# A new order table for a fused gated-linear-attention and gated-MLP kernel

## The chip, the cores and the metric

The kernel runs on one core of a Trainium2 chip. A core has five engines with an instruction queue each: TensorE (PE; the profile shows its weight loads apart, as PEld), VectorE (DVE), ScalarE (ACT), GpSimd (POOL) and SyncE (SP), which here issues the transfers. The metric is the device time of one execution in microseconds (us), as the median of several runs. Beside it one execution was profiled; its time from the first to the last instruction is the span.

## What is computed

The first half is a linear recurrence over 768 steps, for 4 batches and 8 heads of width 48:

```python
for t in range(S):
    state = alpha[:, :, t, :, None] * state + np.einsum('bhd,bhe->bhde', k[:, :, t], v[:, :, t])
    y[:, :, t] = np.einsum('bhd,bhde->bhe', q[:, :, t], state)
```

Its result, with the heads side by side as x (4 x 768 x 384), goes through a gated MLP with a product over the sequence:

```python
h = np.maximum(x @ w_in, 0.0)
u, v = (h[..., :d_ff // 2].copy(), h[..., d_ff // 2:].copy())
v_n = (v - mu) / np.sqrt(var + 1e-06)
v_s = np.einsum('ts,bsd->btd', w_spatial, v_n) + b_spatial[None, :, None]
out = (u * v_s) @ w_out
```

mu and var are taken over the 512 columns of v. All inputs and the output are 32-bit floats; the kernel multiplies in bf16.

## The kernel before

**The recurrence** is done in chunks of 128 steps, 24 of them (6 for each batch), all heads together. For a chunk the kernel takes the logarithm of alpha (ACT, `ln`), sums it up along the steps with a product by a triangle of ones (PE, `cum`, line 618), and forms both exponentials on ACT (`einv`, `eexp`). k is multiplied by one (`kt`, line 642, on POOL or DVE), q by the other (`qt`, line 652, on DVE). PE transposes both (`trk`, line 671), ACT or DVE copies them out of PSUM (`ev`), PE multiplies q and k to scores (`sc`, line 706), DVE masks these (`m`, line 717), and PE multiplies them by v and adds the state's part (`y`, line 734 and 728). The state goes on from chunk to chunk through DVE and POOL (`z`, `S`, `sb`). The first eight chunks are done as four pairs of chunks with functions of their own (`pair`): there the steps are called `lnp`, `cump` (line 406), `totp` (line 423), `einvp`, `eexpp`, `ktp` (442), `qtp` (449), `tr` (470), `updq` (505), `sc` (535), `m` (546), `ya` (562), and a transfer brings 384 KB in place of 192.

**The MLP** takes over when a chunk is through. Its rows are copied (`xs`), transposed (`xt`), copied out (`xe`). Then PE computes `v` (x by one half of w_in, 512 columns), and for each half batch of 384 rows `u` (the other half, transposed), all of them in line 780. DVE or ACT takes v's statistics (`bn`, `rs`) and normalises it (`vn`, line 877 on DVE, 886 on POOL). PE multiplies by w_spatial (`s`, two parts of three products), DVE adds the bias (line 928, tile vsb), POOL or DVE multiplies by u (`g`, line 941, tile gT), PE multiplies by w_out (`o`), ACT or DVE copies the result (line 148 or 150) and SP stores it (line 999). The very last product of the table's numbering comes in two half-width pieces (`oh`, line 963), one of which ACT stores (line 972). For the last `s` of all, line 921 multiplies by u straight from PSUM.

**What sets the order.** No engine decides at run time. The functions only collect operations: each has a key, the engines that can do it, what it needs, and a function that emits it. Then `replay` walks through the string PLAN (line 57): one word for each of 1160 operations, with the letter of the engine that does it (P, D, A, G for POOL, S for a transfer's issue, Q for the transfer itself) and its number. Each engine gets its instructions in the order of the words and works through them strictly in that order; semaphores make it wait where data or a buffer are not there. So the table decides two things: which of its possible engines does an operation, and what stands behind what in each engine's queue. A planner outside the kernel wrote it.

Numbers behind a P word's colons are columns of filler: products of a constant tile (`junk`, line 138) that go out ahead of that operation into the bank that it will use, and whose results are never read.

```python
for word in plan.split():
    number, *junk = word[1:].split(":")
    op, eng = ops[int(number)], LETTERS[word[0]]
    fill.extend(int(x) for x in junk)
    op.emit(eng)
```

The weights come by six transfers of 768 KB (w_in in two halves, w_spatial in three parts, w_out) through two raw buffers, and are cast in pieces to bf16 (line 150 on DVE and POOL, 148 on ACT): a raw buffer's next transfer waits for these casts. Loads of q, k, v and alpha go through three buffers each, in SP's order.

Of the kernel before, what the change touches and what calls it, by code (L numbers as in the profile page):

```python
# [54 lines left out]
LETTERS = {"P": "PE", "D": "DVE", "A": "ACT", "G": "POOL", "S": "SP", "Q": "DMA"}  # L55

PLAN = """
S110 Q111 D0 D17 D5 G47 Q48 D3 D6 D1 S49 Q50 D11 D2 D15 S53 Q54 D13 D12 G14 D4 A118 S51 Q52 G16 A57 S55 Q56 P119:192:64:128:192:320:192:192:64 G9 P58 S114 Q115 G8 A59 P68:64 A60 D61 S112 Q113 A69 P129:256 D62 A120 P70 G72 A71 S180 Q181 A130 P66:384 D73 A121 P64:64 D63 P131 A80 A74 S116 Q117 D123 A132 P79:64 A65 D134 A67 P127 S182 Q183 P75 A141 D81 D122 P138:128 G82 P77 A139 P265 D78 A76 S184 Q185 G18 A266 D84 P125:128 A128 P87 A126 P90 D88 A188 P148 G133 D92 S19 Q20 P199:64:128 A124 D89 P189 G135 A200 G85 D91 S186 Q187 P136:256 G83 P201 D149 P140 A202 G203 D150 A211 S325 Q326 A190 P93 A137 D142 P97 A191 G192 D204 A94 P206:64:128 D193 P208 A98 G143 P95 A209 P195 S24 Q25 P99 G144 A96 D145 D100 P197:64 D196 G22 P151 A198 P267 A207 D153 G21 A23 P215 D152 P218 G86 A268 S327 Q328 P104 D217 G146 P154 A105 D219 G147 S329 Q330 P155 A194 P101 D216 G205 A156 D7 P159 D220 G10 A102 P210 D160 A333 P221 S29 Q30 D212 P157 D103 P161 S331 Q332 G213 P222 A158 P344 A223 G214 P163 D162 A345 D106 G28 P224 P226 A164 P346 D225 G27 P334 A347 D227 P174 G26 A107 D165 P228 A356 P230 A175 G109 S33 Q34 D229 A335 S386 Q387 P166 D176 A336 G348 P245 D349 A177 P233 D338 G337 A246 P170 A231 D167 P243 G31 A171 D232 P353 A32 P340 G178 P351 D234 P239 A354 S37 Q38 A244 P342 D235 P172 A240 S388 Q389 G350 A341 P168 G339 D173 A352 A343 G179 A236 P247:64 S390 Q391 P250 A169 D248 P366 D108 A251 P241 A252 D367 S392 Q393 G35 A249 P355 A242 D368 G238 A394 P253 P363 D254 A255 P395 D357 P273 D237 A397 G358 A396 D365 P281 A36 D360 P282 S432 Q433 D364 A40 P274 D283 S41 Q42 G398 P277 A399 D275 P278 S428 Q429 D400 G39 P256 P262 D279 P402 A258 G359 A264 P269 D276 A403 A404 P270 G284 A257 A263 S430 Q431 A401 P259 P409 D261 P369 D260 G361 D271 P373 P293 A374 D411 P285 S499 Q500 D280 P294 D370 P375 P405 S465 Q466 G45 D410 P297 G272 P298 D406 S467 Q468 A436 P286 A376 G407 D299 P371 G362 P437 D295 A372 P380 A438 D43 D287 A439 A441 P412 G440 S434 Q435 P289 A381 D442 P290 A413 G300 S471 Q472 P444 P414 S469 Q470 P377 G296 A473 D416 D415 D445 A446 P426 A507 D291 G46 S501 Q502 P420 A378 D382 G408 P451 S503 Q504 A443 G44 P474 D421 P508 A427 P447 D379 A476 P417 S596 Q597 A509 G480 A475 D452 P309 A478 G477 S505 Q506 A418 D453 P301 A511 D479 P424 S598 Q599 G510 A310 D448 P454 A302 S600 Q601 A425 P422 D512 G288 A383 D455 P481 A423 P514 G449 D482 P456 A483 P305 D457 G292 A515 D419 A516 P484 A458 S602 Q603 A306 P488 D485 P517 A604 D490 P459 G486 S667 Q668 A513 D519 G450 P605 A460 P313 S669 Q670 D489 G487 A606 P317 D518 A607 A609 G608 S630 Q631 A314 P491 D461 P520 A492 S709 Q710 G611 P321 D610 A521 G384 D318 P493 S632 Q633 P612 A495 D494 P522 A462 P615 D613 P496 D523 A614 D524 G464 A675 D322 P532 A497 P525 S634 Q635 D533 A498 D385 P619 A526 D616 S713 Q714 P534 D463 A527 P536 D621 S671 Q672 A638 P538 D528 A717 P548 D620 A529 S711 Q712 P676 A535 P718 D531 P639 A677 D530 S673 Q674 P544 A719 D537 G679 P622 A720 A640 P549 D539 S636 Q637 A641 A678 A722 P545 G642 D550 A680 P564 D723 S715 Q716 A643 P565 G617 A623 D681 P552 S751 Q752 D546 G721 P553 D644 S781 Q782 G618 D566 P624 P683 A625 P646 D684 G551 P556 A645 D648 S747 Q748 P557 A626 D554 A647 G547 A685 P649 S749 Q750 A682 D558 P653 P690 D650 P725 D655 S785 Q786 P540 G651 A726 A727 D691 P560 G652 A789 P561 D654 G555 A724 P541 D692 P686 S783 Q784 G567 P568 D687 D542 P693 S753 Q754 A755 G559 P656 D562 A694 P569 A657 S877 Q878 G688 P756 D570 P695 G543 P658 A757 P732 D696 S883 Q884 D697 A758 P790 A760 D734 P627 G689 A659 A660 A791 D761 S787 Q788 P580 A793 D733 G792 A628 P728 S881 Q882 P661 D729 D730 G759 P735 D794 A662 P572 D581 A736 G731 D663 A885 P796 P737 S879 Q880 P763 G571 A739 P698 A738 D797 A764 D573 A765 S915 Q916 P701 G563 D798 P740 D629 S911 Q912 A702 G762 A699 P770 G892 P799 A664 D772 S990 Q991 P766 G795 A741 P584 D771 G665 S917 Q918 P886 A585 D801 P576 A887 S913 Q914 D767 P588 A888 A890 D800 G889 A742 P705 D577 A589 G768 P773 D891 P896 G769 D706 A774 P707 S590 Q591 A919 D666 P775 S948 Q949 P893 A776 D777 P802 A708 D894 S1027 Q1028 P592 A895 D897 A700 G926 P703 S950 Q951 D593 A803 P900 A998 D743 P804 P778 A805 D902 A806 S992 Q993 A744 P807 D901 A779 G746 S952 Q953 P817 A704 D780 A956 P815 S994 Q995 G898 A808 P999 D745 G899 P957 A816 D809 P819 A959 A958 S1029 Q1030 P821 A818 D960 P825 A1001 A810 S954 Q955 P813 A1000 D812 A961 P920 D811 S1065 Q1066 P829 A1003 D962 A922 P830 A921 D1004 S1061 Q1062 A820 P826 G923 D831 A814 P822 A1035 D827 S996 Q997 P903 G832 A924 D823 P930 P833 A904 D931 A963 G828 P834 D925 D932 P905 P927 S1031 Q1032 G1002 A906 P964 D835 A928 P967 A966 P849 D965 S1033 Q1034 A929 D907 P850 D836 S1063 Q1064 D968 P1006 D824 P971 G969 A1007 P934 D851 A1069 P908 G970 A1008 D972 P1036 A909 P853 D1005 D973 A1037 P841 A1038 A854 D935 G1039 P1009 A1040 P842 S855 Q856 D936 S594 Q595 P837 G933 D1041 S311 Q312 P937 D1010 S1067 Q1068 P838 D843 A938 G1042 P1070 D839 P1043 A1071 P1013 D1045 P939 A1073 P845 G1072 D1014 A940 A1044 P846 D1074 G1011 P974 D1015 P861 G844 A975 D847 A941 P1076 A862 D910 P976 G848 P1046 A1077 P1016 A977 A978 D1078 P942 A1017 G1075 D1047 G1012 P1018 P1050 D1019 A1020 P1079 A943 D1051 G840 P986 D1080 P857 D1048 P1021 D1081 G1049 P979 D1052 A1022 G852 P1082 A987 D858 P1053 D944 S859 Q860 P988 A1054 S307 Q308 P865 A1083 D980 S574 Q575 A945 S863 Q864 P1084 D1023 P1055 P984 A1085 G946 S586 Q587 A989 P982 S303 Q304 A1057 D1056 A866 D1086 D981 S315 Q316 P869 S582 Q583 P1087 A1024 A983 P1095 D1025 A1088 D947 P1058 D1026 A985 D1089 P1093 A1059 P1097 A1096 D870 P1101 A1094 D1060 S871 Q872 A1098 P1109 S319 Q320 P1105 A1090 S867 Q868 P873 D1091 D1092 P1121 P1106 P1102 D1107 P1122 D1103 P1113 D1108 P1114 D1123 P1117 D1115 G1124 P1110 D1104 P1099 G1116 P1118 D1111 A1100 P1125 A874 D1119 G1112 P1126 S875 Q876 P1129 S323 Q324 D1127 G1120 S578 Q579 P1130 P1132 D1131 G1128 P1140 A1133 P1152 S1134 Q1135 D1141 P1144 A1153 S1142 Q1143 P1136 A1145 S1154 Q1155 P1148 S1146 Q1147 D1137 P1156 S1138 Q1139 A1149 A1157 S1150 Q1151 A1158 Q1159
"""


# [1065 lines left out]
```

## Time and profile before

| what | value |
|---|---|
| median of 3 runs | 139.31 us (139.02 to 139.58) |
| span of the profiled execution | 137.4 us |
| PE busy | 132.7 us, 97% of the span |
| DVE busy | 116.1 us, 84% |
| ACT busy | 101.3 us, 74% |
| POOL busy | 92.9 us, 68% |
| filler on PE (line 138) | 11.4 us busy in 44 records |
| transfers | 28.64 MB, 208 GB/s on average |
| mean granted clock of PE | 0.995 |

How to read what the prediction quotes. A row of a group has the line, engine and operation, what it writes and reads with its shape and count, then busy us and mean ns of one; behind a second bar stands the engine's idle time ahead of these instructions and what ended it. A row of the timeline has the start and the length in us, then the same names; x3 at its end are three instructions merged. Products on PE overlap, so the time of one record is longer than the pace at which they follow one another. A row of the chain of waits has the start, the length and the work that held the end of the program at that time.

### The profile page before, as it was taken

What the parts mean: (1) busy time and instruction counts of PE and PEld (TensorE: products, weight loads), DVE (VectorE), ACT (ScalarE), POOL (GpSimd) and SP (SyncE); (2) the same over time, 40 slices, a digit from 0 to 9 for tenths busy, and PEclk for the clock granted to TensorE, in tenths of its full rate; (3) what the DMA queues carried; (4) which work ended last, traced back from release to release, by engine and by line L of the source; (5) the groups of instructions that cost most, each with busy time, mean ns of one, the idle gap of its engine ahead of it and who ended that gap; (6) DMA issues with size and microseconds to landing.
All of it is one profiled execution on the core that took longest, in us unless ns stands there. A gap on an engine that the chain in (4) does not pass through costs nothing.

```text
span 137.4 us, 5023 instructions
## 1 busy us (share of the span) xinstructions
PE 132.7 (97%) x1943; PEld 88.4 (64%) x1943; DVE 116.1 (84%) x278; ACT 101.3 (74%) x286; POOL 92.9 (68%) x165
## 2 busy tenths in 40 slices
PE   6999999999999999999999999999999999999990
PEld 6768885757667655775667665656666666555660
DVE  7157989998998979998899999989999989878640
ACT  3488687999874799989974887999966757760241
POOL 4734998899894898793399999825666785202910
PEclk9999999999999999999999999999999999999998
DMA  3999999998979899899998989999994602940355
GB/s 95 319 322 328 275 343 328 331 293 243 319 120 314 160 193 203 166 208 193 207 210 160 212 168 199 196 200 212 193 183 114 169 10 108 350 171 6 130 188 197
DMA packets 89000, 28.64 MB, mean 208 GB/s; under 512 B 83728, under 2 KB 87440, under 8 KB 88976
## 3 DMA queue, kind: packets, MB, share of 16 engines
q1 hardware_dynamic: 88800, 28.22, 83.8%
q8 instruction: 15, 0.25, 0.7%
q10 hardware_dynamic: 144, 0.10, 0.2%
q14 instruction: 9, 0.07, 0.1%
q0 software_dynamic: 32, 0.00, 0.0%
HBM read 23.60 MB, written 4.72 MB: 206 GB/s over the span
## 4 chain that ended last, share of the span: by engine, by line
PE 95%; ACT 1%; issue 1%; DVE 0%; ACTq 0%
PE bank L780 58%; PE bank L138 7%; PE bank L671 3%; PE bank L706 3%; PE bank L470 3%; PE bank L734 2%; PE bank L618 2%; PE bank L692 2%; PE bank L535 2%; PE bank L728 2%; PE bank L406 2%; PE bank L343 2%; PE bank L505 2%; PE bank L562 1%; PE bank L320 1%; PE bank L792 1%
## 5 line engine op out<-in xcount | busy, mean ns | idle before, releaser
L780 PE MATMUL bank<-w_spT,vn 128*128 128x384 bf16 x192 | 35.1, 326 | 0.0
L941 POOL TENSOR_TENSOR gT<-vsb,uT 128x384 bf16<-128x384 f32 x25 | 22.8, 928 | 9.2 <-DVE vsb L928 8.6
L780 PEld LDWEIGHTS <-vn 128*128 128x128 bf16 x192 | 17.5, 97 | 10.5
L717 DVE TENSOR_TENSOR ptm<-bank,mask 128x512 bf16<-128x512 f32 x32 | 20.6, 681 | 0.1
L642 POOL TENSOR_TENSOR kt<-kc,binv 128x384 bf16<-128x384 f32 x15 | 13.9, 932 | 9.6 <-ACT binv L630 5.4
L780 PE MATMUL bank<-xT,w_in 128*128 128x384 bf16 x96 | 19.4, 326 | 0.0
L780 PE MATMUL bank<-w_in,xT 128*128 128x512 bf16 x72 | 19.2, 379 | 0.0
L928 DVE TENSOR_TENSOR vsb<-bank,bsp_bc 128x384 f32<-128x384 f32 x31 | 16.6, 552 | 2.0 <-PE bank L780 1.6
L780 PE MATMUL bank<-w_out_sb,gT 128*128 128x384 bf16 (+1 forms) x100 | 18.2, 319 | 0.0
L158 ACT ACTIVATE uT<-bank 128x384 bf16<-128x384 f32 x25 | 11.9, 495 | 5.5 <-PE bank L780 5.5
L150 POOL CAST sbd<-state 64x192 bf16<-64x192 f32 x40 | 13.7, 344 | 2.6 <-DVE state L290 0.5
L845 DVE BATCH_NORM_STATS2 stats<-v_sb 128x6 f32<-128x512 bf16 x20 | 13.7, 686 | 0.2
L148 ACT COPY kqT<-bank 128x256 f32<-128x256 f32 x35 | 11.8, 387 | 2.6 <-PE bank L671 1.7
L158 ACT ACTIVATE v_sb<-bank 128x512 bf16<-128x512 f32 x18 | 10.8, 598 | 3.1 <-PE bank L780 2.6
L290 POOL TENSOR_TENSOR state<-state,bc 128x192 f32<-128x192 f32 x17 | 9.5, 559 | 4.9 <-DVE state L283 2.6
L780 PEld LDWEIGHTS <-w_in 128*128 128x128 bf16 x96 | 8.7, 97 | 6.1
L138 PE MATMUL bank<-junk 128*128 128x64 f32 (+5 forms) x44 | 11.4, 389 | 1.1 <-DVE junk L1012 1.1
L780 PEld LDWEIGHTS <-gT 128*128 128x128 bf16 x100 | 8.9, 97 | 5.4 <-POOL gT L941 0.4
L148 ACT CAST x_sb<-bank 128x384 bf16<-128x384 f32 x20 | 9.4, 490 | 3.3 <-PE bank L734 2.3
L546 DVE TENSOR_TENSOR ptm<-bank,mask 128x512 bf16<-128x512 f32 x16 | 10.0, 682 | 0.5 <-PE bank L535 0.5
L612 ACT ACTIVATE la<-ac 128x384 bf16<-128x384 f32 x16 | 8.4, 533 | 2.5 <-DMA ac<-in_alpha_dram 2.5
L138 PEld LDWEIGHTS bank<-junk 128*128 128x128 f32 x44 | 8.8, 242 | 2.0 <-DVE junk L1012 1.1
(133 smaller groups left out, 290.7 us busy)
## 6 DMA issues: line engine op xcount, KB each, us to landing
ac<-in_alpha_dram SPq DMA_DIRECT2D x16, 192.0 KB, 4.6
kc<-in_k_dram SPq DMA_DIRECT2D x16, 192.0 KB, 4.0
qc<-in_q_dram SPq DMA_DIRECT2D x16, 192.0 KB, 3.9
vc<-in_v_dram SPq DMA_DIRECT2D x16, 192.0 KB, 3.9
raw_w<-in_moe_w_spatial_dram SPq DMA_DIRECT2D x3, 768.0 KB, 4.7
out_dram<-raw_w SPq DMA_DIRECT2D x11, 192.0 KB, 2.0
out_dram<-o_sb SPq DMA_DIRECT2D x9, 192.0 KB, 1.9
ac<-in_alpha_dram SPq DMA_DIRECT2D x4, 384.0 KB, 4.6
```

Source lines behind the costliest of these rows:

```text
L138: nc.tensor.matmul(out=flat[:, 0:cols].rearrange("p (a b) -> p a b", a=4), lhsT=junk, rhs=junk[:, None, 0:n].to_broadcast([128, 4, n]), st ...
L148: nc.scalar.copy(out=out, in_=in_)
L150: ENG[eng].tensor_copy(out=out, in_=in_)
L158: nc.scalar.activation(out=out, in_=in_, func=AF.Relu)
L290: ENG[eng].tensor_tensor(out=st["state"], in0=st["state"], in1=st["bc"][:, :, None].to_broadcast([128, HP, D]), op=ALU.mult)
L546: nc.vector.tensor_tensor(out=st[f"ptm{par}"][:, s], in0=st[f"pt{s}{par}"], in1=mask2[:, par], op=ALU.mult)
L642: ENG[eng].tensor_mul(out=k_blocks(kt3)[:, :, :, 0:D], in0=quad(st["kc"]), in1=st["binv"])
L717: nc.vector.tensor_tensor(out=st["ptm"][:, s], in0=st[f"pt{s}"], in1=mask4, op=ALU.mult)
L780: return lambda ps: nc.tensor.matmul(out=out(ps), lhsT=lhsT(), rhs=rhs(), start=start, stop=stop)
L845: nc.vector.bn_stats(out=stats, in_=d["v_sb"][:, tt, :])
L928: nc.vector.tensor_tensor(out=hold["vs"], in0=ps[:, 0:TH], in1=bsp_bc[:, th, :], op=ALU.add)
L941: ENG[eng].tensor_tensor(out=bt[b]["gT"][:, dsl, cols], in0=hold["vs"], in1=bt[b]["uT"][:, dsl, cols], op=ALU.mult)
```

## The change

PLAN is replaced by another table over the same 1160 operations. Nothing else in the program is different. The new table was planned with the rule that DVE and POOL exclude each other while they multiply two SBUF tensors, and with filler in most of PE's early gaps. The diff is one line of words removed and one added; their beginnings:

```diff
-S110 Q111 D0 D17 D5 G47 Q48 D3 D6 D1 S49 Q50 D11 D2 D15 S53 Q54 D13 D12 G14 D4 A118 S51 Q52 G16 A57 S55 Q56 P119:192:64:128:192:320:192:192:64 G9 P58 S114 Q115 G8 A59 P68:64
...
+D0 G47 D1 D13 G14 D4 D15 D7 S49 Q50 A57 P58:512:512:48 S110 Q111 A118 D17 G18 D3 G16 S51 Q52 A59 S53 Q54 S112 Q113 P68 A69 S114 Q115 S55 Q56
...
```

Of the words, 114 name another engine than before (33 go from DVE to ACT, 33 from ACT to DVE, 20 from POOL to DVE, 17 from DVE to POOL, 6 from ACT to POOL, 5 from POOL to ACT); the others only stand elsewhere. On DVE the evacuations of u go from 7 to 12, those of o from 10 to 7, and the vn from 15 to 12; POOL's vn go from 9 to 12. Filler goes from 22 products of 3200 columns (1344 of them in one block at the start) to 7 of 1936 (1072 at the start, then 112, 240, 448 and 64 ahead of single operations).

PE's queue at the start of the program, before. Here junk is the filler, la the logarithm of alpha of a pair of chunks (108 the second pair, 107 the first), le_pair and lt_pair the triangles:

```order
L138 MATMUL bank_85<-junk 128x192
L138 MATMUL bank_85<-junk 128x64
L138 MATMUL bank_85<-junk 128x128
L138 MATMUL bank_85<-junk 128x192
L138 MATMUL bank_85<-junk 128x320
L138 MATMUL bank_85<-junk 128x192 x2
L138 MATMUL bank_85<-junk 128x64
L406 LDWEIGHTS le_pair
L406 MATMUL bank_85<-la_108,le_pair 128x384
```

and now:

```order
L138 MATMUL bank_85<-junk 128x512 x2
L138 MATMUL bank_85<-junk 128x48
L406 LDWEIGHTS le_pair
L406 MATMUL bank_85<-la_107,le_pair 128x384
L406 LDWEIGHTS lt_pair
L406 MATMUL bank_85<-la_107,lt_pair 128x384
```

The filler block is shorter by 272 columns, and the first cumulative sum behind it is that of the first pair, where it was that of the second.

DVE's queue where w_in arrives, before. ptm is a masked score, kqT a copy of transposed q or k, xT one of the MLP's input, state the recurrence's state:

```order
L285 TENSOR_TENSOR state<-bank_85,state 128x192
L150 COPY xT<-bank_87 128x384
L150 COPY kqT<-bank_90 128x512
L546 TENSOR_TENSOR ptm<-bank_85,mask_118 128x512
L546 TENSOR_TENSOR ptm<-bank_92,mask_118 128x512
L546 TENSOR_TENSOR ptm<-bank_88,mask_118 128x512
L546 TENSOR_TENSOR ptm<-bank_89,mask_118 128x512
L546 TENSOR_TENSOR ptm<-bank_87,mask_118 128x512
L200 MEMSET ones_col 128x1
L546 TENSOR_TENSOR ptm<-bank_90,mask_118 128x512
```

and now:

```order
L285 TENSOR_TENSOR state<-bank_87,state 128x192
L150 CAST w_in_103<-raw_w 128x512
L546 TENSOR_TENSOR ptm<-bank_91,mask_118 128x512
L150 COPY kqT<-bank_90 128x512
L546 TENSOR_TENSOR ptm<-bank_92,mask_118 128x512
L546 TENSOR_TENSOR ptm<-bank_89,mask_118 128x512
L546 TENSOR_TENSOR ptm<-bank_91,mask_118 128x512
L150 CAST x_sb<-bank_92 128x384
L546 TENSOR_TENSOR ptm<-bank_88,mask_118 128x512
L285 TENSOR_TENSOR state<-bank_86,state 128x192
L546 TENSOR_TENSOR ptm<-bank_90,mask_118 128x512
```

DVE now casts one third of w_in's first half, which POOL or ACT did, and six masks stand behind that cast, with a copy, a cast and a state update among them.

DVE's queue at the end of the program, before. vsb is the spatial product with its bias, gT its product with u, raw_w and o_sb are output tiles:

```order
L928 TENSOR_TENSOR vsb_122<-bank_88,bsp_bc 128x384
L928 TENSOR_TENSOR vsb_123<-bank_85,bsp_bc 128x384
L928 TENSOR_TENSOR vsb_124<-bank_87,bsp_bc 128x384
L921 TENSOR_TENSOR gT<-bank_88,uT 128x384
L150 COPY raw_w<-bank_90 128x384
L150 COPY o_sb<-bank_85 128x384
```

and now:

```order
L928 TENSOR_TENSOR vsb_122<-bank_92,bsp_bc 128x384
L928 TENSOR_TENSOR vsb_123<-bank_86,bsp_bc 128x384
L941 TENSOR_TENSOR gT<-vsb_122,uT 128x384
L928 TENSOR_TENSOR vsb_124<-bank_88,bsp_bc 128x384
L921 TENSOR_TENSOR gT<-bank_87,uT 128x384
L941 TENSOR_TENSOR gT<-vsb_124,uT 128x384
L150 COPY raw_w<-bank_85 128x384
```

Two of the last products with u, which POOL did, are DVE's now, one of them behind the direct product. On PE the two half-width output pieces come third and fourth of the last seven output products, where they came third and last, and a whole tile is last.

2 lines of the change are left out of this document (1 added, 1 removed).

## The prediction

> **What bounds the kernel now.** I read the page first, then the busy time by stretches, then the chain of waits in order of time, and last the timelines of the start, of the arrival of w_in and of the end.
>
> ```profile
> span 137.4 us, 5023 instructions
> PE 132.7 (97%) x1943; PEld 88.4 (64%) x1943; DVE 116.1 (84%) x278; ACT 101.3 (74%) x286; POOL 92.9 (68%) x165
> PE 95%; ACT 1%; issue 1%; DVE 0%; ACTq 0%
> ```
>
> TensorE (PE) is busy for 97% of the span and holds 95% of the chain that ended last; no other engine holds more than a hundredth of it. The busy time by stretches (from and to in us, the length, then each engine's busy us and its instructions):
>
> ```profile
> 0.00:6.20 6.20, 5.15 (x17) 4.72 (x18) 3.23 (x20) 2.80 (x3) 3.50 (x14) 1.00 0.73 194
> 6.20:32.00 25.80, 25.43 (x478) 18.86 (x476) 21.61 (x49) 21.73 (x57) 20.46 (x40) 1.00 1.10 322
> 32.00:116.00 84.00, 84.00 (x1332) 54.07 (x1330) 78.59 (x183) 68.27 (x204) 63.20 (x106) 1.00 0.87 181
> 80.00:104.00 24.00, 24.00 (x358) 15.00 (x356) 22.83 (x55) 21.36 (x66) 16.21 (x28) 1.00 0.96 191
> 116.00:137.40 21.40, 18.14 (x124) 10.72 (x121) 12.69 (x29) 8.54 (x25) 5.76 (x7) 0.97 0.50 182
> ```
>
> From 32 to 116 us PE has no idle time: 84.00 us busy out of 84.00. Another order can win nothing there except stalls hidden inside busy records. What is left to win lies ahead of 32 us and behind 116 us. The chain says what PE did there (the first row is the share of each line, the others start, length and work):
>
> ```profile
> by line: PE bank L780 58.1%; PE bank L138 6.6%; PE bank L671 3.2%; PE bank L706 3.1%; PE bank L470 2.7%; PE bank L734 2.3%; PE bank L618 2.2%; PE bank L692 2.2%; PE bank L535 2.0%; PE bank L728 1.8%; PE bank L406 1.6%; PE bank L343 1.6%; PE
> 1.05 5.17 PE bank L138 x16
> 6.22 0.84 PE bank L406 x4
> 20.64 0.76 PE bank L535 x32
> 21.40 0.75 PE bank L780 x3
> 116.64 17.18 PE bank L780 x105
> ```
>
> L138 is the filler. It holds 6.6% of 137.4, 9.07 us: one block of 5.17 us until 6.22, and 3.9 us in small pieces behind that. The first attention product (cumulative sums, L406) starts at 6.22 and the first product with w_in (L780) at 21.40. The last stretch of products runs from 116.64 for 17.18 us, to 133.8. So the profiled time is 6.2 us of start, 3.9 of filler, 0.4 of idle (25.80 less 25.43), 123.3 of products, and 3.6 of end.
>
> **What the change leaves.** In the order PE's list differs by its fillers alone: 3821 rows before, 3806 now, and every other form stands there as often as it did. Fillers go from 22 instructions of 3200 columns to 7 of 1936. Since the 123.3 us of products stay, the sum is made of four terms: the start, the time around w_in's arrival, the middle and the end.
>
> **Start.** Two forms of filler (busy us, then the mean ns of a record), SP's first transfers and ACT's first logarithms:
>
> ```profile
> L138 PE MATMUL bank<-junk 128*128 128x320 f32 x2 | 1.3, 741 | 0.0
> L138 PE MATMUL bank<-junk 128*128 128x384 f32 x2 | 0.9, 528 | 0.0
> 0.74 1.04 SPq L386 DMA_DIRECT2D ac<-in_alpha_dram  x2
> 4.25 0.84 ACT L397 ACTIVATE la<-ac 128x768 bf16<-128x768 f32 x1 [2.23 <-DMA ac<-in_alpha_dram]
> 5.53 0.84 ACT L397 ACTIVATE la<-ac 128x768 bf16<-128x768 f32 x1 [0.44 <-DMA ac<-in_alpha_dram]
> ```
>
> Before, 1344 columns of filler take 5.17 us, 3.85 ns each; the new block has 1072, so 4.1 us, and ends near 5.2. Two alpha transfers are first on SP in both tables, so the first logarithm again ends at 4.25 + 0.84 = 5.09, and the first cumulative sum starts near 5.2 where it was 6.22. This lead of 1.0 us is worth 0.0 by itself, for what comes behind it hangs on transfers.
>
> **The arrival of w_in.** SP's list has the same eleven 384 KB transfers ahead of the first w_in, in another order (kc ahead of qc, vc of pair 0 behind kc and qc of pair 1). So w_in lands when it did:
>
> ```profile
> 20.06 1.17 POOL L150 CAST w_in<-raw_w 128x512 bf16<-128x512 f32 x2
> 20.43 3.69 DVE L546 TENSOR_TENSOR ptm<-bank,mask 128x512 bf16<-128x512 f32 x6
> 20.60 0.64 ACT L148 CAST w_in<-raw_w 128x512 bf16<-128x512 f32 x1
> 21.33 0.82 PE L780 MATMUL bank<-w_in,xT 128*128 128x512 bf16 x3
> ```
>
> Before, POOL casts two thirds one after the other (to 21.23) and ACT the last (to 21.24); the product follows at 21.33. Now POOL, ACT and DVE cast one third each. If they start between 19.7 (an estimate: 0.4 before POOL's start) and 20.06, the product follows at 20.4 to 20.8, a lead of 0.5 to 0.95 us; I take 0.75. Against it stands what PE has not done by then: two score products of pair 2 (L535 x32, 0.76 us) lay ahead of the first w_in product and now lie behind it. 0.75 - 0.76 is 0.0: at the same time as much work is left.
>
> From there PE hardly idled before, so it can only lose. DVE casts w_in ahead of six masks. They took 3.69 us from 20.43; now they start near 20.9 with a copy, a cast and a state update between, and the last ends near 25.0 in place of 24.1. PE has two w_in products (0.75 each) and two cumulative sums (0.84) ahead of the product that reads that mask: 2.3 us of cover for 0.9. POOL casts w_in ahead of the state casts (sbd) for which pair 1's second products wait. For such waits I take +0.15, with -0.4 (the best lead kept, the 0.4 of idle gone, less some wait) and +0.9 (DVE's delay bare) as ends.
>
> **The middle.** The exclusion concerns products of two SBUF tensors. These are the rows of gT on both engines (min, median and max ns), and two evacuations that move:
>
> ```profile
> L941 POOL TENSOR_TENSOR gT<-vsb,uT x25: 910/916/1231, 40.3 to 130.2; 128x384 bf16<-128x384 f32 x25
> L941 DVE TENSOR_TENSOR gT<-vsb,uT x6: 544/550/1175, 40.5 to 126.7; 128x384 bf16<-128x384 f32 x6
> L160 DVE TENSOR_SCALAR uT<-bank 128x384 bf16<-128x384 f32 x7 | 3.7, 545 | 0.4 <-PE bank L780 0.4
> L877 DVE TENSOR_SCALAR vn<-v_sb,mvs,rstd 128x512 bf16<-128x512 bf16 x15 | 5.9, 421 | 1.8 <-ACT rstd L870 1.8
> ```
>
> The medians lie at the minima: few of these were stretched, and PE idled for none. So the new rule buys 0 on the path. The order gives DVE twelve evacuations of uT for seven (5 x 0.545 = +2.7 us) and three vn fewer (-1.3). Between 80 and 104 us DVE is busy for 22.83 of 24, so little of this finds room there. I take +0.1; the ends are -0.4 (as much hidden stall gone as the idle seen ahead of 32 us, an estimate) and +1.4 (all of DVE's surplus on the path).
>
> **The end.** DVE's and ACT's last work, and the stores' time to landing:
>
> ```profile
> 127.68 1.03 DVE L928 TENSOR_TENSOR vsb<-bank,bsp_bc 128x384 f32<-128x384 f32 x2
> 130.34 0.56 DVE L921 TENSOR_TENSOR gT<-bank,uT 128x384 bf16<-128x384 f32 x1 [0.58 <-PE bank L780]
> 133.85 0.70 ACT L148 COPY raw_w<-bank 128x384 f32<-128x384 f32 x2 [0.82 <-PE bank L780]
> 134.58 0.38 ACTq L972 DMA_DIRECT2D out_dram<-raw_w  x1
> out_dram<-o_sb SPq DMA_DIRECT2D x9, 192.0 KB, 1.9
> out_dram<-raw_w ACTq DMA_DIRECT2D x1, 96.0 KB, 1.9
> ```
>
> A whole output tile is last now, where half a one was: one copy of about half a us and a store of 1.9 replace two copies in 0.70 and a store of 1.9: +0.05. The half tiles are earlier, and they need all four blocks of gT, of which DVE writes one last, behind the direct product (L921, then L941). Behind PE's last spatial product that is about 0.1 to release, 0.47 (the pace of 1.03 for two), 0.55, and 0.1 again: 1.2 us. PE covers it with two whole output tiles, 8 x 0.164 = 1.3 us (17.18 for 105). It just fits, and one more delay breaks it. In all I take +0.15, with 0 and +0.6 (a gT of 1175 in place of 550).
>
> By the Trainium skill (SBUF — State Buffer, "SBUF: two separate sides") a VectorE operation with two SBUF inputs and a GpSimd operation that reads SBUF exclude each other for a whole instruction; the trace agrees where 1175 stands beside 544. By that rule DVE's earlier gT would wait here for one of POOL's, and the end would be some +0.45, for 140.0 in all.
>
> **Sum.** 0.0 + 0.15 + 0.1 + 0.15 = +0.4 us. The profiled span of 137.4 becomes 137.8; the median of the runs is 139.31, so 1.9 us lie around the span, and the forecast is 139.7 us. About 0.5%, 0.7 us, is what a measurement of this kernel can tell from no change: the forecast is one that it can't.
>
> **Rivals.** *The filler was real time (faster).* The small pieces shrink from 1856 columns to 864, 2.1 us less at the old 3.9 for 1856. If the scores that were put off fit into that time, the lead at w_in's product is 0.95 and nothing new waits, the time is 139.3 - 1.0 = 138.3. For it: those pieces lay in the chain. Against it: work was put off, and the transfers come no earlier. 0.20.
>
> *PE stays slow for longer (slower).* 320 columns of filler in the first block take 741 ns, 384 columns later 528: PE ran slowly at first. The new block is 1.1 us shorter, and behind it PE waits for logarithms and exponentials with little filler. If the slow pace lasts until pair 1's sums are through and some us on, two pairs' cumulative sums (0.84 each two) cost 1.7 more and the small products with them about 0.9, an estimate. Of these 2.6 us the 2.1 of filler saved hide most; 0.5 stay, so 140.2. It decides where rows behind 6.5 us still show the slow pace. 0.12.
>
> By the Trainium skill (TensorE: Matmul & The Clock Gate, "What's actually happening") about 3.4 us of sustained work open the clock, counted in a window that runs free. By that rule a block of 4.1 us may miss a whole window; no run shown here has one so short.
>
> *VectorE becomes the wait (slower).* If the surplus of 1.4 us falls into the stretch from 80 to 104, masks come late, products wait, and the chain grows by as much: 140.7. For it: 1.17 us of room there. Against it: the order spreads these evacuations. It decides where DVE's work in that stretch passes 24 us. 0.18.
>
> **Numbers.** The forecast has 0.50: 0.46 of it within 0.7 us of 139.3, 0.02 on either side. Faster: 0.20 + 0.02 = 0.22. Slower: 0.18, 0.10 of the slow start, and 0.02: 0.30. Same: 0.48, the other 0.02 of the slow start in it. The range is 138.4 (some of the first rival left out) to 140.9 (just above the last).
>
> **What would show it.** Right: w_in's first product near 20.6 with 32 score products behind it, PE without idle from 32 to 116, PE's end within 0.5 us of where it was. Wrong: idle on PE behind 32 us, the slow pace behind 6.5, w_in cast well before 19.7, or dense products unbroken from much before 28 us.

## The result and the profile after

The new table is a little slower: 140.23 us (median of 20 runs) beside 139.22 (20 runs). The medians are 1.0 us apart; the ratio, 1.0059 with a 95% interval of 1.0035 to 1.0083, puts the loss at 0.8 us. Executions more than 1.5% above the fastest of the same kernel are left out of the ratios, here and below. From here on *before* and *after* are the two tables.

The page of after: span and instructions, the engines' busy time, and the shares of the chain that ended last.

```profile
span 138.4 us, 4947 instructions
PE 130.3 (94%) x1901; PEld 82.9 (60%) x1913; DVE 118.3 (86%) x281; ACT 101.4 (73%) x285; POOL 94.3 (68%) x166
PE 73%; DVE 9%; SPq 8%; DMA 4%; ACT 2%; issue 2%; POOL 1%; POOLq 0%; DVEq 0%; ACTq 0%
```

The span is 1.0 longer. PE held 95% of the chain of before; now it holds 73%, and DVE 9%, which had less than 1%. The stretches of after:

```profile
6.20:32.00 25.80, 23.44 (x449) 15.71 (x450) 22.88 (x51) 22.04 (x61) 17.73 (x35) 1.00 1.12 331
32.00:116.00 84.00, 82.75 (x1309) 53.63 (x1316) 79.85 (x184) 67.75 (x198) 64.79 (x108) 1.00 0.92 203
80.00:104.00 24.00, 23.73 (x352) 15.05 (x353) 22.59 (x54) 20.60 (x62) 17.68 (x31) 1.00 0.99 210
```

PE now idles for 1.25 us between 32 and 116, where it had none. Part of that is no idle: 12 of the 72 products of L780 with 512 columns have no record in this trace. So the loss is read off another way: when the same product ends in both traces, set against the products that PE has done by then, counted at the paces at which they follow each other in both.

| mark | before | after | lost up to here |
|---|---|---|---|
| first cumulative sum of chunk 8 ends | 36.83 | 37.86, with 0.94 us more products done | 0.09 |
| attention of chunk 23 ends | 114.85 | 117.02, with 1.32 more | 0.85 |
| last product of the program ends | 134.14 | 135.01 | 0.87 |
| span | 137.4 | 138.4 | 0.95 |

The product of the first mark, in the timeline of before and then of after (start and length in us):

```profile
36.50 0.34 PE L618 MATMUL bank<-la,ut_ones 128*128 128x384 bf16 x1
```

```profile
37.53 0.33 PE L618 MATMUL bank<-la,ut_ones 128*128 128x384 bf16 x1
```

Up to 37 us nothing much was lost, then 0.76 until 117, and behind that 0.10. Where w_in arrives, after does what was forecast. The three casts and the first product with w_in, in the timeline of after:

```profile
19.45 0.62 ACT L148 CAST w_in<-raw_w 128x512 bf16<-128x512 f32 x1
19.45 0.43 DVE L150 CAST w_in<-raw_w 128x512 bf16<-128x512 f32 x1 [0.24 <-DMA raw_w<-in_moe_w_in_dram]
19.48 0.86 POOL L150 CAST w_in<-raw_w 128x512 bf16<-128x512 f32 x1
20.40 0.81 PE L780 MATMUL bank<-w_in,xT 128*128 128x512 bf16 x3
```

Behind 38 us the chain shows where the end was set. Its pieces in after from 73 to 79 us (start, length, work):

```profile
73.19 0.56 DVE vsb L928
...
74.00 2.16 DVE ptm L717 x4
...
76.32 0.54 DVE vsb L928
76.86 0.26 DVE state L285
77.12 0.47 DVE vsb L928
77.59 0.60 DVE gT L941
78.19 0.48 DVE vsb L928
```

For nearly all of 5.5 us the end hung on DVE's queue. By the ends of consecutive products PE waited here for 0.13 (at 73.5), 0.11 (74.1) and 0.19 us (79.1), and elsewhere for 0.14 (41.9) and 0.18 (111.1); ahead of 38 us it waited 0.41 at the transposes of w_spatial (L792, 35.8), without which after would have stood 0.32 better than before there. Before had four waits over 0.04 us behind 38, 0.29 in all.

All of these waits of after, but for the one at 111.1, end when an operation of DVE does. At 111.1 PE waits for POOL: the transposes of kt start 0.06 us behind the end of POOL's second kt (110.89), here and in the traces of x9, x13 and x14 below. In the timeline of after:

```profile
108.99 1.90 POOL L642 TENSOR_TENSOR kt<-kc,binv 128x384 bf16<-128x384 f32 x2
...
110.95 0.29 PE L671 MATMUL bank<-ident,kt 64*128 64x64 bf16 x8
```

What stands ahead of two of these waits, in the timeline of after: DVE and POOL at the same time.

```profile
33.37 1.24 DVE L150 CAST vbp<-vc 128x384 bf16<-128x384 f32 x2
33.39 1.00 POOL L150 CAST w_row<-raw_w 128x768 bf16<-128x768 f32 x1
34.86 0.87 DVE L150 COPY w_spT<-bank 128x384 bf16<-128x384 bf16 x3
35.78 0.35 PE L792 MATMUL bank<-ident,w_row 64*128 64x64 bf16 x12 [0.27 <-DVE w_spT L150]
...
71.94 2.10 POOL L941 TENSOR_TENSOR gT<-vsb,uT 128x384 bf16<-128x384 f32 x2 [0.35 <-DVE vsb L928]
72.11 1.16 DVE L642 TENSOR_TENSOR kt<-kc,binv 128x384 bf16<-128x384 f32 x1
```

The same operations by minimum, median and maximum (ns), in after:

```profile
L941 POOL TENSOR_TENSOR gT<-vsb,uT x24: 907/916/1260, 39.7 to 129.8; 128x384 bf16<-128x384 f32 x24
L642 POOL TENSOR_TENSOR kt<-kc,binv x14: 912/916/1225, 38.6 to 109.9; 128x384 bf16<-128x384 f32 x14
L941 DVE TENSOR_TENSOR gT<-vsb,uT x7: 541/548/799, 45.2 to 131.6; 128x384 bf16<-128x384 f32 x7
L642 DVE TENSOR_TENSOR kt<-kc,binv x2: 548/854/1159, 53.8 to 72.1; 128x384 bf16<-128x384 f32 x2
L290 DVE TENSOR_TENSOR state<-state,bc x2: 734/742/750, 18.0 to 109.4; 128x192 f32<-128x192 f32 x2
L150 DVE CAST vbp<-vc x2: 348/662/977, 33.4 to 33.6; 128x384 bf16<-128x384 f32 x2
```

Two of these rows in before:

```profile
L290 DVE TENSOR_TENSOR state<-state,bc x3: 348/408/605, 80.3 to 113.0; 128x192 f32<-128x192 f32 x3
L150 POOL CAST vbp<-vc x4: 506/509/512, 15.1 to 33.4; 128x384 bf16<-128x384 f32 x4
```

One kt takes 1159 in place of 548, one cast 977 in place of 348, the state updates 742 where before had one at 348. So the exclusion that the table was planned with did not keep the two engines apart on the chip. Before had collisions as well (gT of 1175 in place of 544, at 40.5 us), but PE shows no wait behind those.

### The profile page after: what moved, and what is told of

Same layout as the page of the kernel before. It is cut to its first block, busy times and chain, and to the rows that moved or that the text cites. A ratio compares the mean times of both kernels' runs of the same rounds, so it can differ in the third digit from the quotient of the medians.

```text
span 138.4 us, 4947 instructions
## 1 busy us (share of the span) xinstructions
PE 130.3 (94%) x1901; PEld 82.9 (60%) x1913; DVE 118.3 (86%) x281; ACT 101.4 (73%) x285; POOL 94.3 (68%) x166
## 4 chain that ended last, share of the span: by engine, by line
PE 73%; DVE 9%; SPq 8%; DMA 4%; ACT 2%; issue 2%; POOL 1%; POOLq 0%; DVEq 0%; ACTq 0%
PE bank L780 51%; SPq L386 8%; DMA kc<-in_k_dram 4%; PE bank L706 3%; PE bank L671 3%; PE bank L734 2%; PE bank L692 2%; PE bank L618 2%; PE bank L728 2%; DVE ptm L717 2%; PE bank L343 1%; DVE vsb L928 1%; DVE stats L845 1%; PE bank L562 1%; DVE vbp L150 1%
## 5 line engine op out<-in xcount | busy, mean ns | idle before, releaser
L780 PE MATMUL bank<-w_spT,vn 128*128 128x384 bf16 x192 | 35.1, 326 | 0.1
L780 PEld LDWEIGHTS <-vn 128*128 128x128 bf16 x192 | 17.4, 97 | 10.6
L717 DVE TENSOR_TENSOR ptm<-bank,mask 128x512 bf16<-128x512 f32 x32 | 20.4, 679 | 0.0
L780 PE MATMUL bank<-xT,w_in 128*128 128x384 bf16 x96 | 18.8, 326 | 0.0
L780 PE MATMUL bank<-w_out_sb,gT 128*128 128x384 bf16 (+1 forms) x100 | 18.4, 319 | 0.0
L780 PE MATMUL bank<-w_in,xT 128*128 128x512 bf16 x60 | 16.9, 379 | 1.1 <-issue 0.2
L158 ACT ACTIVATE v_sb<-bank 128x512 bf16<-128x512 f32 x20 | 11.7, 593 | 2.5 <-PE bank L780 2.5
L780 PEld LDWEIGHTS <-w_in 128*128 128x128 bf16 x96 | 8.8, 97 | 6.2 <-DVE xT L150 0.2
L780 PEld LDWEIGHTS <-gT 128*128 128x128 bf16 x100 | 8.7, 97 | 4.8 <-DVE gT L941 0.2
L148 ACT CAST x_sb<-bank 128x384 bf16<-128x384 f32 x18 | 8.5, 482 | 3.3 <-PE bank L734 2.3
L158 ACT ACTIVATE uT<-bank 128x384 bf16<-128x384 f32 x20 | 9.5, 493 | 1.5 <-PE bank L780 1.5
L886 POOL TENSOR_SCALAR vn<-v_sb,rstd,nb 128x512 bf16<-128x512 bf16 x12 | 9.3, 772 | 1.2
L780 PEld LDWEIGHTS <-xT 128*128 128x128 bf16 x72 | 6.1, 98 | 5.7 <-ACT xT L148 0.4
L148 ACT COPY o_sb<-bank 128x384 f32<-128x384 f32 x7 | 3.3, 478 | 7.9 <-PE bank L780 7.9
```

The lines of the kernel that those rows point to most:

```text
L148: nc.scalar.copy(out=out, in_=in_)
L158: nc.scalar.activation(out=out, in_=in_, func=AF.Relu)
L717: nc.vector.tensor_tensor(out=st["ptm"][:, s], in0=st[f"pt{s}"], in1=mask4, op=ALU.mult)
L780: return lambda ps: nc.tensor.matmul(out=out(ps), lhsT=lhsT(), rhs=rhs(), start=start, stop=stop)
```

## Experiments

Three theories. *Collisions*: DVE is late where its SBUF operations overlap POOL's and are stretched, and PE waits for it. *Load*: DVE has too much to do since the evacuations of uT moved there. *Order*: PE's own sequence is worse, whatever DVE does. Later two questions on the start joined: what the filler does (cover, real time, or the clock), and whether the start's lead is worth anything. Each kernel was timed beside runs of before on the same chip (medians 139.17 to 139.51). "Clock" is the number of executions with a mean granted clock under 0.99.

| kernel | median us | ratio to before (95%) | PE's last product ends | clock |
|---|---|---|---|---|
| after | 140.23 | 1.0059 (1.0035 to 1.0083) | 135.01 | 5 of 20 |
| x1, vbp on POOL | 140.34 | 1.0040 (1.0018 to 1.0062) | 134.28 | 2 of 12 |
| x2, gT late | 140.94 | 1.0114 (1.0090 to 1.0139) | 135.67 | 0 of 5 |
| x3, both | 140.53 | 1.0077 (1.0050 to 1.0105) | 134.82 | 4 of 11 |
| x6, uT on ACT | 140.54 | 1.0094 (1.0069 to 1.0120) | 135.32 | 0 of 6 |
| x9, vbp on POOL, kt earlier | 139.36 | 1.0014 (0.9986 to 1.0042) | 134.17 | 2 of 12 |
| x10, x9 with the old filler | 141.88 | 1.0190 (1.0154 to 1.0225) | 136.90 | 0 of 6 |
| x4, before with the new filler | 141.06 | 1.0101 (1.0069 to 1.0134) | 137.26 | 3 of 11 |
| x5, after with the old filler | 142.69 | 1.0227 (1.0195 to 1.0259) | 137.51 | 0 of 6 |
| x11, after, old first block | 140.07 | 1.0055 (1.0031 to 1.0079) | 134.81 | 1 of 11 |
| x12, before, new first block | 139.79 | 1.0022 (0.9991 to 1.0052) | 133.93 | 0 of 12 |
| x13, x9 with two edits more | 139.45 | 1.0008 (0.9984 to 1.0033) | 134.88 | 0 of 12 |
| x14, after with two fillers more | 140.04 | 1.0050 (1.0022 to 1.0078) | 134.77 | 0 of 12 |

(One execution of x3, at 702 us, is no time of this program and is left out of its ratio.) Before has 1 of 89.

### x1: the vbp casts back on POOL

```diff
-P250 D350 P247 D339 A36
+P250 G350 P247 G339 A36
```

> The kernel after, with pair 3's two casts vbp on GpSimd again (one letter each). In the trace of after they lie on VectorE from 33.37 for 1.24 us, one of them 0.98 us long where the fastest of its form takes 0.35, while GpSimd casts w_row from 33.39; TensorE then waits 0.41 us at the w_spT transposes (L792) near 35.8. Collision theory (TensorE lost its 0.8 us in waits for VectorE where VectorE's SBUF operations are stretched beside GpSimd's): that wait falls below 0.15, TensorE's last product ends 0.2 to 0.4 earlier than 135.0, the time is 139.8 to 140.0 beside 140.2. Load theory (VectorE has too much work, 118.3 us busy): VectorE is relieved of 1.2 us and the same is gained. Order theory (TensorE's products stand in a worse order, whatever VectorE does): the wait stays, 140.2.

The timeline of x1 at the same place:

```profile
32.85 0.82 POOL L150 CAST w_row<-raw_w 128x768 bf16<-128x768 f32 x1
33.62 1.02 POOL L150 CAST vbp<-vc 128x384 bf16<-128x384 f32 x2
35.01 0.52 PE L792 MATMUL bank<-ident,w_row 64*128 64x64 bf16 x24
```

The 24 transposes that after did in two halves, with the wait between them, are one record again: the 0.41 is gone, and so is the 0.14 at 41.9. PE's last product ends 0.73 earlier, of which 0.15 was there ahead of this place already. The waits from 73 us on stayed as they were. The median did not fall with the profiled execution, which was the fastest of the twelve; over all executions the ratio is 0.2% lower, inside the interval. Both theories expected this gain, so x1 alone does not choose between them.

Five traces with vbp still on DVE gave a scale for the collision without being made for it, since POOL's cast started at slightly different times in each:

| trace | stretched vbp cast, ns | it ends behind POOL's cast by, us | end to end over the wait in L792, ns |
|---|---|---|---|
| after | 977 | 0.21 | 459 |
| x6 | 922 | 0.21 | none here; 0.22 us of wait ahead of the first of these transposes |
| x2 | 859 | 0.21 | 344 |
| x11 | 794 | 0.21 | 275 |
| x14 | 489 | 0.21 | none |

DVE's cast does not run slower, it waits: whenever POOL's cast ended, it was through 0.21 later. In after, x2 and x11, with the same operations of DVE ahead, PE's wait follows the cast: 118 ns less of cast is 115 less of wait, 65 less is 69 less, and at 489 (x14) there is none. In after POOL's own cast took 1005 ns, in the other four 822 to 827, so the collision can hold both sides. By the Trainium skill (SBUF — State Buffer, "SBUF: two separate sides") the port pair that DVE and POOL share is an exclusive lock for a whole instruction, and a DVE operation contends for it with two SBUF inputs or in a 2-port performance mode; that the cast is held until POOL's is through agrees. A cast has one input, so by that rule it would be in such a mode, which no trace here shows.

### x2 and x3: POOL's two gT behind the state update

```diff
-D566 G567 A626 ... P649 G547 P690 ... D650 A726 D691 D692 P560 S323 Q324 G651 D654 D655 G652
+D566 A626 ... P649 P690 ... D650 A726 D691 D692 P560 S323 Q324 G651 D654 D655 G652 G567 G547
```

> The kernel after, with two gT products of GpSimd (batch 1) put behind its next state update and casts, so that they no longer run beside VectorE's kt of chunk 15 (72.11, 1.16 us where the other kt takes 0.55). No engine changes, VectorE's list is the same word for word. Collision theory: kt takes 0.55 to 0.6, TensorE's waits at 73.5, 74.1 and 79.1 (0.13, 0.11, 0.19) go, its last product ends 0.2 to 0.4 earlier, the time is 139.8 to 140.0. Load theory: VectorE's work is the same and nothing is gained, 140.2. Order theory: 140.2.

The timeline of x2, with the kt and what followed it:

```profile
71.86 0.55 DVE L642 TENSOR_TENSOR kt<-kc,binv 128x384 bf16<-128x384 f32 x1
...
76.60 0.56 DVE L928 TENSOR_TENSOR vsb<-bank,bsp_bc 128x384 f32<-128x384 f32 x1 [0.88 <-POOL gT L941]
...
79.01 0.81 PE L780 MATMUL bank<-w_in,xT 128*128 128x512 bf16 x2 [0.53 <-DVE vsb L928]
```

The collision was gone (0.55), PE had no wait at 73.5 and 74.1, and behind them it stood 0.24 better against after than ahead of 73. Then the edit's own price came: a late gT keeps the vsb that it reads, DVE waited 0.88 for that buffer with everything behind it in its queue, and PE waited 0.38 and 0.59, and 0.40 once more at 116. The first half of the expectation came true, the sum did not; as a fix the edit is worthless. But DVE's list is the same word for word, so the 0.24 is the collision's alone. The same two edits together:

> The kernel after with both edits, the vbp casts on GpSimd and the two gT products behind the state update. Collision theory: 0.5 to 0.7 us of the 0.8 come back, 139.5 to 139.7, TensorE's last product near 134.4. Load theory: the vbp part alone, 139.9. Order theory: 140.2.

x3 shows the sum of both: no wait at L792, none at 73.5, and x2's new ones near 79.

### x6: the uT evacuations back on ACT

```diff
-D242 ... D427 ... D535 ... D818 ... D814 ... D987 ... D1094 ... D1096
+A242 ... A427 ... A535 ... A818 ... A814 ... A987 ... A1094 ... A1096
```

> The kernel after with the eight evacuations of uT that went from ScalarE to VectorE back on ScalarE; the three that went the other way stay on ScalarE too, so VectorE has four. VectorE is relieved of 8 x 0.53 = 4.2 us, ScalarE has 8 x 0.43 = 3.4 more. Load theory: the lost 0.8 comes back, 139.4 to 139.6. Collision theory: the collisions at 33.4, 72.1 and 109.4 are not touched; -0.2 to +0.3, 140.0 to 140.5. Order theory: 140.2.

DVE was relieved (114.9 us busy in place of 118.3) and the kernel is not faster: 1.0094. The waits at 73.5, 74.1, 79.1 and 111 stood as in after. At L792, where DVE had one evacuation less ahead of the stretched cast (922 ns), the wait was 0.22 in place of 0.41: there the stretch and the added evacuation made the wait together. That is nearly all that the relief gained. ACT, with more to do, became late in its turn, and from 95 us on x6 is behind after. The timeline of x6:

```profile
95.34 0.32 PE L618 MATMUL bank<-la,ut_ones 128*128 128x384 bf16 x1 [0.32 <-ACT la L612]
```

So the load theory falls as an account of the 0.8 us: 3.4 us less work on DVE gained about 0.2.

### x9: vbp on POOL, and kt started ahead of POOL's gT

```diff
-D566 G567 A626 ... P653 D721 S992
+D721 D566 G567 A626 ... P653 S992
```

(with x1's two letters)

> The kernel after, with the vbp casts on GpSimd, and VectorE's kt of chunk 15 two evacuations earlier in its list, ahead of the vsb on which GpSimd's gT waits, so that VectorE's operation has started when GpSimd's does. Collision theory: kt takes 0.55 to 0.6, TensorE's waits at 35.8, 41.9, 73.5, 74.1 and 79.1 go; its last product ends near 133.9 to 134.2 (135.0 in after, 134.3 with vbp alone), fast executions at 139.1 to 139.3. Load theory: VectorE's work falls by the stretch alone, TensorE's waits near 73 to 79 stay, 134.3. Order theory: nothing beyond the 0.45 that vbp gave at the w_spT transposes, 134.3.

In the timeline of x9 the kt runs ahead of the gT, and a good part of its stretch is gone:

```profile
70.91 0.67 DVE L642 TENSOR_TENSOR kt<-kc,binv 128x384 bf16<-128x384 f32 x1
72.12 1.79 POOL L941 TENSOR_TENSOR gT<-vsb,uT 128x384 bf16<-128x384 f32 x2 [0.96 <-DVE vsb L928]
```

The chain of x9 in the same stretch as shown of after:

```profile
72.41 0.55 PE bank L706 x16
72.96 0.23 PE bank L671 x16
73.19 2.06 PE bank L780 x12
75.25 0.20 PE bank L692 x8
75.45 0.49 PE bank L780 x3
```

PE all the way, to 79.97. The waits at 35.8, 41.9, 73.5, 74.1 and 79.1 are gone; what is left is the one near 110 (0.18). PE's last product ends 0.84 earlier than in after, and the median, 139.36, is level with before (ratio 1.0014, 0.9986 to 1.0042), where after's interval begins at 1.0035. Two engine letters and one word's place carry about 0.6 of the 0.8 us.

PE's list is word for word that of after, so the order theory falls too, and the two traces can be set against each other product by product. Behind w_in's first products x9 is 0.16 later than after. Then it gains at five places and at no other: 0.43 at L792, 0.14 at 41.9, and 0.13, 0.11 and 0.19 behind 73, 1.00 in all. The edit takes the kt out of the collision and also brings it 1.2 us earlier, so x9 does not divide the last three between the two; x2 gives the collision 0.24 of them.

### x4 and x5: the fillers exchanged

x4 is before with the filler of after, x5 after with that of before; the block at the start of each, then the pieces at the same operations.

```diff
-P119:192:64:128:192:320:192:192:64
+P119:512:512:48
```

> The kernel before, with the fillers of the kernel after: a first block of 512, 512 and 48 columns, then 112, 240, 448 and 64 ahead of the same products as there; 1936 columns in place of 3200, and no other word changed. The filler was real time (the rival of the prediction): 2.1 us of small pieces less in the chain, 138.3. The filler only covers waits that last until w_in lands near 19.5 (the forecast): the first w_in product stays within 0.2 of 21.4, 139.1 to 139.5 beside 139.3. Clock theory (with little filler TensorE's granted clock is not full in some executions): most executions at 139.1 to 139.5, but some with a mean granted clock under 0.99 and 1 to 2.5 us more; of the 42 executions of before so far none was under 0.995, of the 20 of after five were.

> The kernel after, with the fillers of the kernel before (3200 columns: the block of 1344 and the small pieces ahead of the products that they preceded there). The filler was real time: 1 to 2 us slower than after, 141 to 142. Cover: w_in's first product stays near 20.4 and TensorE's waits ahead of it shrink by about the filler's time, 139.9 to 140.3. Clock theory: no execution with a mean granted clock under 0.99, the spread of the times as narrow as that of before, the median 0.2 to 0.4 lower than that of after.

In neither did the filler merely cover waits. Before with the other filler is slower, 1.0101. The profiled execution is one of the three with a low clock; the stretches of x4 (the granted clock is the third number from the end):

```profile
8.00:10.00 2.00, 1.59 (x26) 1.27 (x26) 1.68 (x4) 1.89 (x7) 0.91 (x1) 1.00 1.17 321
10.00:12.00 2.00, 1.67 (x43) 1.55 (x43) 1.72 (x5) 1.62 (x7) 0.12 (x1) 0.76 1.17 325
12.00:14.00 2.00, 2.00 (x12) 1.34 (x10) 0.26 (x2) 0.65 (x2) 1.85 (x4) 0.50 1.17 325
14.00:16.00 2.00, 1.99 (x23) 0.93 (x22) 1.31 (x3) 1.71 (x5) 1.94 (x4) 0.89 1.17 338
```

The clock was full and fell to half: 0.96 us of the first 2, all of the next, 0.44 of the third, 3.4 us in all. From 4 to 8 us PE had been busy for 2.35 of 4, in before for all 4.00. By the Trainium skill (TensorE: Matmul & The Clock Gate, "What's actually happening") the gate judges windows of about 3.4 us; the 3.4 agrees. But x4's executions with a full clock also have a median of 141.03. These have no trace; the trace of the slow clock points at the new pieces. Set against before product by product, it is 0.21 us ahead until the clock falls, and then the pieces of 240 and 448 columns put it back by 0.95 and 1.08 us (at half clock), at a place where PE in before is busy for all of 10 to 16 us. So x4 does not show what before would be with less filler: it took pieces out and put others where this order has no gap.

In after the old filler is real time: 142.69 in place of 140.23, 1.7% (ratios to before 1.0227 and 1.0059). The first product with w_in, in the timeline of x5:

```profile
22.87 0.81 PE L780 MATMUL bank<-w_in,xT 128*128 128x512 bf16 x3
```

20.40 in after. The pieces stand ahead of products that in this order have no gap there, and the lateness is handed on. x10 says the same of the kernel with both fixes:

> The same as the kernel with vbp on GpSimd and kt earlier, and with the fillers of the kernel before. If collisions explain what the profile shows and the fillers what the spread of the times shows, this is level with before: 139.0 to 139.4, with no mean granted clock under 0.99. If the order itself is worse: 139.7 to 140.1.

It has the 2.5 us of x5, not the time of before.

### x11 and x12: the first block alone

> The kernel after, with the first block of fillers of the kernel before (1344 columns for 1072), its other four fillers kept. The first cumulative sum starts about 1.0 later. The prediction (this lead is worth 0.0, since what comes behind hangs on transfers): w_in's first product stays near 20.4, 140.0 to 140.4. Chain theory (the start of this order is one chain of TensorE, ScalarE, VectorE and GpSimd from the first sum on, and the transfers have slack): w_in's first product comes 0.8 to 1.3 later and the time is 141.0 to 141.5.

> The kernel before, with the first block of fillers of the kernel after (1072 columns for 1344), all its small pieces kept. The first cumulative sum starts 0.8 to 1.0 earlier. The prediction (worth 0.0): w_in's first product stays within 0.2 of 21.4, 139.0 to 139.4. Chain theory, if it holds for this order too: 0.5 to 1.0 earlier, 138.3 to 138.8, faster than both kernels. Clock theory: with the small pieces in place the granted clock stays full, where the kernel with all the new fillers showed 0.50 from 12 to 14 us.

In x11 the pairs' cumulative sums end 0.88 later than in after, and at 16.3 PE is still 0.65 late. At the transposes of kt near 18.6 the lateness is gone, and w_in's product comes when it did. The timeline of x11:

```profile
18.59 0.40 PE L470 MATMUL bank<-ident,kt 128*128 128x128 bf16 x4
...
20.41 0.81 PE L780 MATMUL bank<-w_in,xT 128*128 128x512 bf16 x3
```

The chain of after says what those transposes hang on:

```profile
11.75 5.74 DMA kc<-in_k_dram
17.62 0.93 POOL kt L442
```

A transfer of k that lands at 17.49, and the kt made from it: PE waits 0.73 for it in after, and a start that is later by less than that costs nothing. 140.07 beside 140.23: the block's length is worth nothing here, as the prediction said, and the 2.5 us of x5 come from the small pieces. x12 is not told apart from before either (1.0022, 0.9991 to 1.0052), and with the small pieces in place no execution lost its clock, which suggests, but does not show, that in before the pieces hold it.

### x13 and x14: filler put where the trace shows gaps

```diff
-P77:240 ... P195
+P77:352 ... P195:256
```

(x14 is after with this; x13 is x9 with this and output tile o of batch 2, number 858, on ACT behind A975.)

> The kernel with vbp on GpSimd and kt earlier, and two edits more: the evacuation of output tile 1 of batch 2 on ScalarE behind its next cast, since TensorE waits 0.18 for VectorE's at 110.3, and filler in two gaps of TensorE that the trace shows, 112 columns more at 10.1 (gap 0.37) and 256 at 18.7 (gap 0.73). Collision theory with the waits of the page: 0.0 to 0.2 less than the 139.36 of that kernel, TensorE's last product near 134.0. Clock theory: no execution with a mean granted clock under 0.99, of which that kernel had two in twelve. If the filler is not hidden: 0.3 to 0.7 more.

> The kernel after, with filler in two gaps of TensorE that its trace shows: 112 columns more ahead of 10.1 (gap 0.36) and 256 new ones ahead of 18.6 (gap 0.71). No other word changed. So far 14 of 77 executions with the new fillers at the start (after and six kernels made from it) had a mean granted clock under 0.99 and were 1 to 2.5 us longer than the others of the same kernel; the one kernel with these two fillers had none in twelve; before has one in 92. Clock theory: none of some twelve executions under 0.99, the median 139.8 to 140.1, the collisions' 0.6 to 0.8 still there. If the filler has nothing to do with it: two or three of twelve under 0.99, median 140.2.

Neither fill costs time, and none of the 24 executions had a clock under 0.99, against 14 of 77 of after and the six kernels that have its pieces. The kernels ran on different chips; on the one that timed both kinds it is 1 of 11 (x11) and 0 of 12 (x13), so the filler as the reason is likely but not shown. (The expectation's "one in 92" for before counted 20 executions whose clock is not recorded; it is 1 of 89 with the last runs.) x14's median, 140.04, equals that of after's executions with a full clock, 140.09. Its trace has the waits behind 73 and at 111 as after has; at L792 it has none, since POOL's cast there happened to start earlier (489 ns in the table above), but 0.32 at 38.9 in its place. x13 is level with before and with x9. The wait near 111 that its evacuation on ACT was meant for is still there, 0.19: it was for POOL's kt and not, as the expectation has it, for DVE's evacuation. Its profiled execution, at 140.06, shows a wait of 0.60 us at 39.0 that x9 does not have; seven of its twelve executions lie at 139.1 to 139.5, so most seem to be without it. What makes it is not settled. No version beats before.

## Why the prediction was right or wrong

The forecast was 0.4 us more, 139.7; measured were 0.8 (0.5 to 1.2 by the interval), 140.2. That is in the range and on the side where the sum pointed, just past the 0.5% that the text set as "no change". Read off the traces the loss is 0.95 us of span, and by terms the nearness is in part luck: the arrival was 0.45 better and the middle 1.07 worse than its term, and the two partly cancel.

**Start, 0.0: right,** and for the reason given: x11 is late at the sums and on time at the transposes behind the k transfer.

**w_in's arrival, +0.15: measured -0.3,** inside its ends of -0.4 and +0.9. The lead (20.40 for 21.33, 0.93 where 0.75 was taken) and the 32 scores behind it came about as worked out, though the casts started at 19.45, ahead of the 19.7 that the text took as earliest. Of the waits that the 0.15 was taken for little came: from 20.4 to 35.7 PE is idle for 0.44 us, 0.27 of it at L792.

**The middle, +0.1: this is the term that failed.** It measured 1.17 (from -0.32 ahead of the wait at 35.8 to 0.85 at 117); the upper end of +1.4 held it. The text's own sign for wrong, idle on PE behind 32 us, is there, and its sign for right, PE's end within 0.5 us of where it was, is missed with 0.87. The waits for DVE that x9 takes away make 1.00 of the 1.17. The working said that the exclusion buys 0, since the rows of gT were hardly stretched, and that five uT and three vn change DVE's list. Giving the uT back brought about 0.2 (x6). What cost were moves that the working did not price at all: the vbp casts of pair 3 and the kt of chunk 15, which went from POOL to DVE and there met POOL's next SBUF operation. It asked what the absence of collisions would buy, and not whether the new table brings collisions of its own; every operation that changes sides between these two engines should have been looked up for what the other engine does at that moment.

**The end, +0.15: right.** It measured 0.10, and PE has no wait in its last stretch.

**Rivals.** "The filler was real time" is not decided for before: x4, with less of it but at other places, is slower, and x12, with a shorter block alone, is level. The gain that it forecast did not come. "VectorE becomes the wait" had the right engine and the wrong condition: DVE's work from 80 to 104 is 22.59 of 24, less than before, and PE waits for it at 36, 42, 74 and 79. What decided was less the amount of work than when a single operation is held. "PE stays slow for longer" did not occur at the start (the granted clock is full from 5.8 us in after), but a relative did: five of twenty executions have a mean clock under 0.99, and the median of the others is 140.09 in place of 140.23. That is the smaller part of the loss. Where the clock falls in those five no trace shows; in x4 it fell at 11 us.

## What to carry to other kernels

When a table, a scheduler or a hand moves SBUF-to-SBUF work between VectorE and GpSimd, list every moved operation, casts too, and look up what the other engine runs at that time and who waits for the moved one; a collision with slack is free (gT in before), one on an engine with a full queue reaches the engine that waits for it (a cast held for 629 ns cost PE 0.41 us). A planner's rule holds in the planner's time: here the table was planned to keep the two engines apart and a kt met a gT all the same, so look in the trace whether the rule came true before crediting it. Filler belongs in gaps that the trace of the same order shows; the filler of before cost 1.7% in after, and that of after cost 1.0% in before.

## What the runs showed of the hardware

A cast of f32 to bf16 on VectorE with one SBUF input is held until GpSimd's cast is through and ends 0.21 us behind it, whether it had taken 489 or 977 ns by then (five traces). In one trace (x4) TensorE's clock fell to half for 3.4 us, some 3 us behind a stretch in which it was busy for 2.35 of 4 us and no idle time was longer than 0.83; 368 columns of filler more, hidden in gaps, went with none in 24 executions under 0.99 where the kernels without them had 14 of 77.
